# New engine orders for a two-layer attention and token-mixing kernel: the planner's DMA constants and its correction tables are replaced

## The chip, the cores and the metric

The kernel runs on one core of a Trainium2 chip. The metric is the device time of one execution in microseconds (us). Times are compared as medians of several executions. One execution was also recorded by the hardware profiler. Its "span" runs from the first to the last instruction of the program, and its own time is a little longer than its span.

## The reference, cut to what matters

Two different blocks are applied in turn, A then B, twice over (two layers with the same weights), each as a residual on a layer norm of x. Block A is attention with 32 heads of width 16 in a sliding window of 256 tokens. Block B normalises once more and mixes along the tokens: its matrices act on the token axis (2048 to 1792 and back), with a gelu between.

```python
x = x + A(_layernorm(x), wqkv, wo)        # x: 1 x 2048 x 512, bf16
x = x + B(_layernorm(x), w1, b1, w2, b2)
x = x + A(_layernorm(x), wqkv, wo)
x = x + B(_layernorm(x), w1, b1, w2, b2)
# A: H = 32, Dh = 16, W = 256
scores = einsum("bhqd,bhkd->bhqk", q, k) * Dh ** -0.5
mask = (i - j >= 0) & (i - j < W)
o = einsum("bhqk,bhkd->bhqd", softmax(where(mask, scores, -1e9)), v) @ wo
# B
u = gelu(einsum("bsd,sf->bdf", layernorm(x), w1) + b1)
y = transpose(einsum("bdf,fs->bds", u, w2) + b2)
```

## The kernel before, in words

The 2048 tokens lie in SBUF as 16 tiles of 128 tokens (t0 to t15), in four chunks of four tiles (m = 0 to 3). `STEPS` names the stages of a layer and the order in which their operations are created: p (norm, transposes, q, k and v of a chunk), a (attention of a chunk), w (output projection of a chunk), u (a chunk's share of the first token matrix) and U (the last share, with the gelu). The second token matrix, y, of layer 0 is created together with p of layer 1, so that dense matmuls of one block can stand between the attention work of the other. The y of layer 1 comes last, with the stores of the output.

Attention of a chunk is done for four groups of eight heads (o = 0 to 3). This document names such a head group by layer, chunk and group: 0.a3.o2 is layer 0, chunk 3, group 2. For each group TensorE makes four or five score pieces (line 851), ScalarE takes the exponential of each piece in two halves (863), VectorE masks them (876, 879), and TensorE multiplies with v and sums the denominators in the same matmuls (896, called pv here). Then comes a round trip that is the heart of this case, since most of it is DMA:

- VectorE copies the two PSUM banks to `cs` (940, two copies).
- SyncE (SP) issues a DMA that gathers the denominators into `rr` (942) and four DMAs that move half of the sums up by 16 partitions (946, "up").
- VectorE takes the reciprocal in `rr` (949).
- SP writes it to DRAM, `rscr` (951), and reads it back spread over partitions as `md` (954).
- GpSimd multiplies sums and reciprocals into `oT` (958).
- TensorE uses four such `oT` of a chunk in the output projection (968), and VectorE adds that to x (972).

The last group of chunk 3 takes another way without DMA (909, 923 to 927). So there are 30 round trips of seven DMAs in all.

GpSimd also makes the masked copies `kbd` of k that the scores read (783, two halves for each group, from the staging tile `stg`), small pieces of v (813), and two steps of each layer norm: `rstd` (694) and its power (696), before VectorE normalises (700). The weights of the token matrices stream in: w1 in 56 loads of 256 KB (`load_w1`, 983), used by the u matmuls (1014); w2 in 112 loads of 128 KB (`load_w2`, 994), used by the y matmuls (1037), whose result is added to x (1042).

What sets the order: every operation is created with a cost, and `schedule` plays all five engines forward on these costs. `_pick` chooses for an engine among the operations that are ready. `HOLD` and `WINDOW` decide how long TensorE prefers scores and pv over dense matmuls, and `RANK` shifts the priority of each dense matmul group (`fprio`). For a DMA the planner takes three numbers: `issue` (how long the SP queue is held), `cost` (its share of a common transfer time) and `lat` (from there to the landing). `schedule` also gives out the buffers of each pool, in its own order, and picks VectorE or ScalarE for some copies out of PSUM (`evac`, lines 734 and 736). Then `reorder` moves operations within each engine by the table `MOVES`, one list for each of TensorE, VectorE, ScalarE, GpSimd and SP. `emit` writes the queues with the waits that the data and the buffers need.

So the five queues are fixed lists. Each engine takes its list strictly in order, and an instruction that waits for a DMA holds everything behind it on that engine. In particular a reciprocal (949) that waits for `rr` holds all of VectorE, a multiply (958) that waits for `md` or an "up" holds the `kbd` and `rstd` work behind it on GpSimd, and a DMA whose input isn't ready holds all later DMAs on SP.

Of the kernel before, what the change touches and what calls it, by code (L numbers as in the profile page):

```python
# [16 lines left out]
W2F, W2OUT = 2, (3, 7)  # L17
# [4 lines left out]
    38, 478, -248, -93, 7, 6, -38, -55, 0, -12, 14, -1, -14, 17, 7, 49, 0, 0, -11, -57, -29, 12, -32, 17, 163, -113,  # L22
    -26, 0, -76, 48, 174, -114, 0, -155, 72, 0, 0, 91, 0, -197, -108, 0, -146, 0, 0, -43, -29, -200, 193, 102, 0,
    116, -16, 0, -1, 11, -60, 21, -73, 18, 2, -2, 7, 89, 40, -31, -47, -15, 10, 0, -22, -49, 42, 322, -14, 6, 33, 2,
    0, 13, 12, 0, -17, -8, -15, 0, 5, -20, 0, 0, 0, -65, 142, 93, 62, -58, 23, 23, -51, -8, -30, 20, 27, 0, -36,
    -55, 10, 8, 0, 76, 151, 136, 83, -40, -3, -176, 115, -122, 460, -486, -53, -30, 29, 53, 0, -45, 0, 0, -39, -32,
    -78, 0, -2, 0, 0, 0, 0, 0, -52, 0, 0, 0, 0, 0, 0, 0, 19, -6, -13, -12, 0, -6, 4, -18, 0, 0, 7, 132, -19, -10,
    -13, 10, 103, -116, 115, -193, 419, 0, 41, 10, 1, 0, -10, 6, -14, -46, 5, -20, 0, 0, 103, -15, 11, 17, 0, 0, -6,
    -79, -112, -156, 0, -7, 0, -468, 0, 0, 0, 2, 0, 17, -7, 9, 6, 12, 0, -28, 0, 45, 117, 31, -17, 0, 0, 0, -19, -6,
    -107, -186, 167, -24, 82, 120, 248, 217, 122, 0, -3, 18, 55, -4, -27, 0, -6, 0, -120, 0, 1, 50, 52, 478, 268, 0,  # L30
    13, 47, 0, -11, 0, 113, 15, 46, 44, -30, -22, -52, 0, 14, -410, 20, 180, -153, -435, -439, 359, -7, 0, -3, 15,
    -10, 13, 10, -4, 12, 0, -86, -10, -52, -43, 17, 227, -51, -403, -135, -167, -266, -230, -240, 44, 0, 0, 4, -190,
    72, 0, 0, 0, 0, 3, 0, -1, 0, 0, 0, 0, 0, 0, 0, 0, 0, 0, 0, 0, 0, 0, 0, 0, 0, 0, 0, 0, 0, 6, 57,
# [15 lines left out]
        0, 0, 0, 0, 0, 0, 0, 0, 0, 0, 0, 0, 0, 0, 0, 0, 0, 0, 0, 0, 0, 0, 0, 0, 0, 0, 0, 0, 0, 0, 0, 0, 0, 0, 0, 0,
        0, 0, 0, 0, 0, 0, 0, 0, 0, 0, 0, 0, 0, 0, 0, 0, 0, 0, 0, 0, 0, 0, 0, 0, 0, 0, 0, 0, 0, 0, 0, 0, 0, 0, 0, 0,  # L50
        0, 0, 0, 0, 0, 0, 0, 0, 0, 0, 0, 0, 0, 0, 0, 1, -1, 0, 0, 0, 0, 0, 0, 0, 0, 0, 0, 0, 0, 0, 0, 0, 0, 0, 0, 0,
        0, 0, 0, 0, 0, 0, 0, 0, 0, 0, 0, 0, 0, 0, 0, 0, 0, 0, 0, 0, 0, 0, 0, 0, 0, 0, 0, 0, 0, 0, 0, 0, 0, 0, 0, 0,
        0, 1, -1, 0, 1, -1, 0, 1, -1, 0, 0, 0, 0, 0, 0, 0, 0, 0, 0, 0, 0, 0, 0, 0, 0, 0, 3, -1, -1, -1, 4, 0, -2,
        -1, 2, 0, -3, 0, 0, 1, -1, 1, -1, 3, -1, 2, -2, -2, 0, 2, -1, -1, 3, -1, 2, 2, -3, 6, 6, -5, -2, -2, -2, 2,
        2, -4, 1, 4, 0, 0, 2, -1, 1, 1, 1, 1, 1, -15, 1, -1, 3, 3, 3, 20, 3, 3, 0, -7, 1, -8, -8, 16, 7, -3, 1, 1,
        15, 0, 2, 5, -9, 11, -4, -11, -11, -11, -1, -6, 0, 0, 0, 2, -10, 2, -8, 4, 11, -3, 2, -3, 1, -4, -4, 0, 4,
        6, -2, 2, -6, 6, 6, -6, -2, -1, 9, -2, -10, -3, 1, 12, -3, -3, 2, -3, 8, 2, -5, -2, -6, -3, -2, -2, 1, -3,
        5, 0, -2, -1, -1, -1, 0, 0, 0,
    ),
    (  # L60
        7, 4, 4, -2, -4, 6, 6, 6, -4, 5, 6, 4, 7, 7, 3, -7, 2, 4, 4, 4, 4, 4, 5, 10, 24, 1, 3, 13, 3, 5, 0, 1, 4,
        -30, 5, 7, -8, -28, 8, 2, -2, -6, 1, 13, -7, -1, 1, 8, -3, 5, -1, -41, -2, -2, -2, 4, -54, 3, 8, 4, -2, 4,
        -1, -1, 3, 11, -9, 4, 1, -1, 4, -7, 1, 6, 1, 6, 4, 5, -25, -1, 3, 4, 5, 6, 0, 3, 4, 4, 4, -3, 3, 3, 4, -23,
        4, 4, 4, 0, -3, 2, 2, 2, 2, -26, -32, 1, 2, 2, 2, -2, -5, 1, -1, 2, -1, -1, 0, 1, 1, 1, -3, 0, 0, 0, 0, 0,
        1, -1, 0, 0, 0, 0, 0, 0, 0, 1, -1, 0, 0, 0, 1, 1, -2, 0, 1, 1, 1, 2, 0, -5, 1, -1, 0, 2, -1, -1, 0, 2, 0, 1,
        1, 2, -5, 1, 3, 0, 0, -5, 5, 1, -1, 1, 4, 2, -6, -1, 1, 2, 0, 2, 0, 1, 1, -12, 1, 2, -2, 2, 2, 2, -2, 1, 1,
        -7, 0, 0, 0, 0, 0, 0, 0, 1, -1, 0, 0, 0, 1, 1, 1, -3, 0, 0, 0, 2, 0, 1, -3, 0, 2, 0, 1, 3, -4, 3, 3, -2, 3,
        1, 3, 4, 0, 5, 3, 7, 3, 3, 5, 5, 5, -5, -15, -9, -20, -4, 2, 2, 4, 2, 0, -5, 1, 3, -7, -1, -1, 0, 1, 3, -2,
        -1, -1, 1, -1, 0, 0, 0, 0, 0, 0, 0, 1, -1, 0, 0, 0, 1, 1, -2, 0, 0, 0, 0, 1, -1, 0, 0, 0, 0, 0, 0, 0, 0, 0,
        1, -1, 0, 0, 0, 0, 0, 0, 1, 2, 2, 2, 3, 1, -4, -7, 0, 0, 0, 0, 1, -1, 1, -1, 0, 0, 0, 0, 0, 0, 0, 0, 0, 0,  # L70
        0, 0, 0, 0, 0, 0, 0, 0, 1, -1, 2, 0, 2, 3, 3, -5, -1, 5, 3, 1, 3, -8, 2, -5, 1, -6, 0, 0, 0, 0, 0, 2, 0, -2,
        0, 2, 0, 2, -3, -1, 0, 3, -1, -1, 1, 1, 2, 2, -1, -6, 0, 1, -1, 1, 1, -2, 0, 0, 2, 3, 1, 2, 2, 2, 3, 4, 6,
        6, -10, 8, 10, -5, -13, 1, 7, 7, -1, -7, 8, -11, -9, 7, 5, 7, -6, 6, -7, -4, 4, -13, -5, -2, -8, 0, 0, 1,
        -1, 0, 0, 0, 2, 0, -2, 0, 1, 1, 1, 5, 3, 1, 3, 4, 4, 1, 3, -7, 3, 1, -14, 1, 2, 4, -1, 3, -15, -2, 1, -3, 1,
        -1, 3, -1, 2, -2, 3, 3, -1, -1, -6, 1, 2, 2, -1, 2, 2, 4, -7, 0, 0, 1, 1, 1, -8, 0, 0, 0, 0, 2, -1, -1, 0,
        0, 1, 1, -2, 0, 1, -1, 0, 0, 0, 0, 2, 0, 1, 1, 1, 1, 1, 1, 3, 6, 4, 5, 0, 8, -14, 4, 2, 5, -5, 4, 6, -4, 2,
        5, 6, 6, 3, -17, 5, 5, 2, -22, 3, 6, -9, -8, -16, 4, 5, 7, -2, 6, 6, 7, 0, 7, -9, 6, 6, 0, -5, 0, 4, -17, 1,
        2, 2, -17, -16, 0, 0, 0, 0, 0, 1, -1, 0, 2, -1, -1, 0, 0, 0, 0, 0, 0, 0, 0, 0, 0, 1, 1, 1, 1, 1, 1, 1, 1, 2,
        2, 2, -2, 1, 2, 4, 1, 1, -3, 1, 3, 3, 0, 4, 1, -4, 2, -26, 1, -3, 3, 1, -2, 1, 1, 2, 0, -6, 0, 1, 1, 2, 2,
        2, -5, -3, 2, 0, -2, 2, 2, -2, 1, 1, -4, 0, 0, 2, 0, 1, -3, 3, 0, -2, -1, 0, 0, 0, 0, 0, 3, 1, -1, -3, 2, 0,  # L80
        3, 1, -1, 1, 1, 1, 1, 5, -10, -1, 1, 2, -3, -3, 2, 0, 2, 0, -4, 0, 6, 3, 3, 4, 4, 4, 4, -7, -6, -8, 1, -8,
        0, 0, 0, 0, 0, 9, 13, -1, 18, -2, 0, 0, -3, 2, 2, -10, 2, -9, 2, 3, -8, 2, -5, -10, 3, 4, 4, -6, -3, -1, -6,
        1, 1, -2, 2, -1, 2, 0, -3, 0, 0, 0, 0, 0, 0, 3, 0, 0, -3, 0, 0, 1, 1, 3, -3, 2, -1, -3, 1, -1, 0,
    ),
# [71 lines left out]
class Graph:  # L156
# [158 lines left out]
    HOLD = 300.0  # L315
    WINDOW = ({0: 400.0, 1: 300.0, 2: 50.0}, {0: 100.0, 1: 250.0, 2: 100.0})
# [222 lines left out]
def bass_interleave_layers__sliding_block__mixer_token_mlp__prompt_kernel(  # L539
# [21 lines left out]
    with es:  # L561
# [39 lines left out]
        g = Graph(nc, es)  # L601
# [512 lines left out]
```

The softmax here doesn't subtract the row's maximum and nothing guards it: scores larger than these inputs give would overflow.

## Time and profile before

| what | us |
|---|---|
| median of 6 runs | 487.22 |
| lowest and highest of these | 483.77 and 490.5 |
| the profiled execution, its own time | 483.77 |
| its span | 482.0 |
| TensorE busy | 436.7 |
| VectorE busy | 370.7 |
| ScalarE busy | 323.4 |
| GpSimd busy | 136.6 |

The profiled execution is the lowest of the six: it took 3.45 us less than their median. A working made on its trace explains 483.77 us, and has to be carried over to the median. "Busy" of TensorE counts the time in which at least one matmul is under way. Its mean granted clock was 0.992 of full speed, so there is hardly a general clock loss, but a lower clock in a few places. In the views, PE is TensorE, PEld its weight loads, DVE VectorE, ACT ScalarE, POOL GpSimd, and SPq the issuing of DMAs on SP's queue.

### The profile page before, as it was taken

To read this page: it belongs to the slowest core of one execution; us is meant where nothing else is said; L and a number is where in the kernel's file an instruction comes from. 1 tells how busy PE (TensorE), PEld (TensorE's weight loads), DVE (VectorE), ACT (ScalarE), POOL (GpSimd) and SP (SyncE) were. 2 spreads that over 40 slices of the span, in tenths; PEclk is the share of its full clock that TensorE was granted. 3 is DMA by queue.
4 is the path that set the end of the run, shared out by engine and by line. 5 is a ranking of instruction groups with operands and counts; after the bars stand their busy time and mean duration, and the time that the engine had idled before them with its cause. 6 is when DMAs were issued, how large, how long until landed. Compare 5 with 4: busy or idle time off the path is not lost.

```text
span 482.0 us, 15699 instructions
## 1 busy us (share of the span) xinstructions
PE 436.7 (91%) x6831; PEld 208.9 (43%) x6831; DVE 370.7 (77%) x747; ACT 323.4 (67%) x367; POOL 136.6 (28%) x205
## 2 busy tenths in 40 slices
PE   7898887798888699999999999988999969999997
PEld 4453533343343244444555454434444325444443
DVE  6989978989989977665887889879996846951313
ACT  2899999999989850634878988996999852061000
POOL 4223435234521413024103433532474031200000
PEclk9999999999999999999999999998999999999999
DMA  8602221234344253331225422330345335424655
GB/s 244 183 3 73 61 85 39 65 105 130 87 112 129 59 151 89 88 88 44 78 60 137 116 67 71 89 102 9 101 112 160 83 105 162 127 71 120 175 152 176
DMA packets 83993, 49.47 MB, mean 103 GB/s; under 512 B 14676, under 2 KB 78164, under 8 KB 83924
## 3 DMA queue, kind: packets, MB, share of 16 engines
q1 hardware_dynamic: 83924, 48.46, 35.6%
q8 instruction: 54, 0.88, 0.8%
q14 instruction: 15, 0.12, 0.1%
HBM read 41.43 MB, written 2.59 MB: 91 GB/s over the span
## 4 chain that ended last, share of the span: by engine, by line
PE 63%; ACT 14%; DVE 9%; DMA 7%; SPq 3%; issue 3%; POOL 2%; POOLq 0%
PE PS L1037 18%; PE PS L1014 16%; ACT pt L863 13%; PE PS L767 7%; PE PS L851 6%; PE PS L968 5%; PE PS L896 5%; PE PS L797 4%; DVE cs L940 2%; DMA cs<-cs 2%; DVE pt L879 1%; DMA w1b<-in_B_w_dram 1%; DMA wqkv<-in_A_wqkv_dram 1%; DMA rr<-cs 1%; SPq L946 1%
## 5 line engine op out<-in xcount | busy, mean ns | idle before, releaser
L863 ACT ACTIVATE pt<-PS 128x1024 bf16<-128x1024 f32 (+1 forms) x304 | 284.3, 1032 | 37.6 <-PE PS L851 35.9
L1014 PE MATMUL PS<-xh_sb,w1b 128*128 128x512 bf16 x448 | 107.1, 382 | 6.4 <-DMA w1b<-in_B_w_dram 3.5
L1037 PE MATMUL PS<-ub,w2b 128*128 128x512 bf16 x448 | 103.6, 380 | 0.7 <-ACT pt L863 0.5
L851 PE MATMUL PS<-qT,kbd 32*128 32x64 bf16 (+4 forms) x1632 | 61.0, 244 | 18.9 <-ACT pt L863 8.6
L958 POOL TENSOR_TENSOR oT<-cs,md 128x512 bf16<-128x512 f32 x30 | 39.5, 1316 | 101.4 <-DMA md<-rscr 46.5
L1014 PEld LDWEIGHTS PS<-xh_sb,w1b 128*128 128x128 bf16 x448 | 40.3, 98 | 58.8 <-issue 9.4
L879 DVE TENSOR_TENSOR pt<-pt,ldm 128x1024 bf16<-128x1024 bf16 (+1 forms) x80 | 60.7, 760 | 5.5 <-ACT pt L863 5.2
L767 PE MATMUL PS<-xhT,wqkv 128*128 128x512 bf16 x256 | 63.2, 381 | 0.9 <-DVE cs L940 0.6
L1037 PEld LDWEIGHTS PS<-ub,w2b 128*128 128x128 bf16 x448 | 41.6, 98 | 51.2 <-issue 3.1
L783 POOL TENSOR_SCALAR kbd<-stg,par 128x512 bf16<-128x512 bf16 x56 | 46.3, 836 | 55.2 <-DVE stg L734 50.6
L1026 DVE TENSOR_TENSOR ub<-PS,ub 128x512 f32<-128x512 f32 x70 | 46.0, 682 | 15.9 <-PE PS L1014 15.7
L851 PEld LDWEIGHTS PS<-qT,kbd 32*128 32x128 bf16 x1632 | 23.4, 92 | 73.4 <-ACT pt L863 38.1
L1042 DVE SCALAR_TENSOR_TENSOR x_sb<-PS,bcol,x_sb 128x512 bf16<-128x512 f32 x32 | 23.1, 744 | 39.0 <-PE PS L1037 39.0
L1029 ACT ACTIVATE ub<-ub,bcol 128x512 bf16<-128x512 f32 x28 | 18.5, 713 | 46.8 <-DVE ub L1026 46.6
L940 DVE COPY cs<-PS 128x512 f32<-128x512 f32 x60 | 38.9, 681 | 9.0 <-PE PS L896 8.6
L896 PE MATMUL PS<-pt,vt 64*18 64x64 bf16 (+4 forms) x3040 | 39.6, 243 | 4.6 <-DVE qT L734 1.3
L694 POOL TENSOR_SCALAR rstd<-agg 128x2 f32<-128x2 f32 (+1 forms) x40 | 9.5, 237 | 120.4 <-DVE agg L691 119.4
L689 DVE BATCH_NORM_STATS2 stats<-x_sb 128x6 f32<-128x512 bf16 x64 | 42.6, 680 | 1.1 <-DMA x_sb<-in_A_x_dram 0.5
L876 DVE TENSOR_TENSOR pt<-pt,ldm 128x512 bf16<-128x512 bf16 (+1 forms) x104 | 40.2, 404 | 1.8 <-ACT pt L863 1.3
L896 PEld LDWEIGHTS PS<-pt,vt 64*18 64x18 bf16 x3040 | 31.1, 85 | 15.7 <-DVE pt L876 3.6
L968 PE MATMUL PS<-wo_sb,oT 128*128 128x512 bf16 x128 | 33.0, 389 | 3.4 <-POOL oT L958 2.8
L767 PEld LDWEIGHTS PS<-xhT,wqkv 128*128 128x128 bf16 x256 | 21.7, 98 | 29.9 <-issue 3.2
(54 smaller groups left out, 328.1 us busy)
## 6 DMA issues: line engine op xcount, KB each, us to landing
w1b<-in_B_w_dram SPq DMA_DIRECT2D x56, 256.0 KB, 3.1
w2b<-in_B_w_dram SPq DMA_DIRECT2D x112, 128.0 KB, 2.4
md<-rscr SPq DMA_DIRECT2D x30, 256.0 KB
cs<-cs SPq DMA_DIRECT2D x120, 32.0 KB, 2.7
out_dram<-x_sb SPq DMA_DIRECT2D x16, 128.0 KB, 1.8
x_sb<-in_A_x_dram SPq DMA_DIRECT2D x3, 512.0 KB
wqkv<-in_A_wqkv_dram SPq DMA_DIRECT2D x2, 384.0 KB
x_sb<-in_A_x_dram SPq DMA_DIRECT2D x4, 128.0 KB, 2.4
```

What stands on the lines that cost most here:

```text
L689: op("vector", lambda e, t=t: e.bn_stats(stats[:, t, :], x_sb[:, t, :]), reads=[f"x{t}"], writes=[f"st{t}"], cost=dve_cost(512))
L767: mm_group(ft, 4, lambda e, c: e.matmul(PS[:, ft.slot, :], lhsT=wqkv[:, c, which * 512 + o * P:which * 512 + (o + 1) * P], rhs=xhT[:, tx.s ...
L783: op("gpsimd", lambda e, h=h: e.tensor_scalar(kbd[:, tk[o].slot, :, h, :], stg[:, ts.slot, :].rearrange("p (s n) -> p s n", n=64), par[:, ...
L851: last = e.matmul(PS[:, bank(r), c0 * 64:(c0 + nb) * 64], lhsT=kbd[32 * r:32 * r + 32, tkk.slot, jj, :, :].rearrange("p h n -> p (h n)"), ...
L863: return e.activation(pt[:, tp.slot, 2 * u:2 * u + 2, 0:n], PS[:, b0:b0 + 2, 0:n], ACTF.Exp, scale=SMSCALE)
L879: return e.tensor_tensor(v, v, msk.unsqueeze(1).unsqueeze(1).to_broadcast([P, 4, k, w]), op=ALU.mult)
L896: last = e.matmul(PS[32 * r:32 * r + 18, tO[h].slot, q0 * 64:(q0 + nb) * 64], lhsT=vt[64 * h:64 * h + 64, tvv.slot, jj, 4 * o + r, :], rhs ...
L940: op("vector", lambda e, tO=tO[h], tc=tc, h=h: e.tensor_copy(cs[:, tc.slot, h], PS[:, tO.slot, :]), reads=[tO[h]], writes=[(tc, h)], cost= ...
L968: mm_group(ft, 4, lambda e, o, i=i, ft=ft: e.matmul(PS[:, ft.slot, :], lhsT=oT[:, tos[o][0].slot, i * P:(i + 1) * P], rhs=wo_sb[:, o, :], ...
L1014: out_ = e.matmul(PS[:, tu.slot, :], lhsT=w1b[:, tw.slot, s, tt * P:(tt + 1) * P], rhs=xh_sb[:, 4 * m + s, :], start=(n == 0 and s == 0), ...
L1026: op("vector", lambda e, tu=tu, ft=ft: e.tensor_tensor(uacc(ft), PS[:, tu.slot, :], uacc(ft), op=ALU.add), reads=[tu] + uk(ft), writes=uk( ...
L1037: mm_group(ft, NFT, lambda e, fc: e.matmul(PS[:, ft.slot, :], lhsT=w2b[:, tws[fc // W2F].slot, fc % W2F, k * P:(k + 1) * P], rhs=uT(fc), s ...
```

## The change

No line that computes anything is touched. Three sorts of numbers are replaced:

- The planner's numbers for DMAs, as below.
- `HOLD` and `WINDOW`, as below.
- The tables `RANK` (322 entries, of which 182 differ) and `MOVES` (717, 747, 367, 201 and 409 entries for TensorE, VectorE, ScalarE, GpSimd and SP). Their entries are plain shifts without a meaning of their own.

```diff
-    HOLD = 300.0
-    WINDOW = ({0: 400.0, 1: 300.0, 2: 50.0}, {0: 100.0, 1: 250.0, 2: 100.0})
+    HOLD = 600.0
+    WINDOW = ({0: 400.0, 1: 300.0, 2: 0.0}, {0: 150.0, 1: 400.0, 2: 400.0})
...
                     # rr <- cs
-                   writes=[(tr, 0)], dma=True, cost=300, lat=1400.0, issue=570.0, prio=len(g.ops))
+                   writes=[(tr, 0)], dma=True, cost=200, lat=1400.0, issue=610.0, prio=len(g.ops))
                     # cs <- cs, the four "up"
-                       writes=[(tc, "up", r)], dma=True, cost=120, lat=1600.0, issue=380.0, prio=len(g.ops), after=[o_rr])
+                       writes=[(tc, "up", r)], dma=True, cost=120, lat=1850.0, issue=575.0, prio=len(g.ops), after=[o_rr])
                     # rscr <- rr
-                   writes=[te], dma=True, cost=300, issue=580.0, prio=len(g.ops))
+                   writes=[te], dma=True, cost=200, lat=1500.0, issue=400.0, prio=len(g.ops))
                     # md <- rscr
-                   writes=[tm], dma=True, cost=700, lat=2500.0, issue=590.0, prio=len(g.ops))
+                   writes=[tm], dma=True, cost=700, lat=2650.0, issue=645.0, prio=len(g.ops))
                     # w1b
-               dma=True, cost=1000, lat=2000.0, issue=390.0, prio=1e6 + len(g.ops))
+               dma=True, cost=1000, lat=1900.0, issue=450.0, prio=1e6 + len(g.ops))
                     # w2b
-                    cost=340 * W2F, lat=1700.0, issue=390.0, prio=1e6 + len(g.ops), after=w2_sent[-W2OUT[g.layer]:][:1]))
+                    cost=340 * W2F, lat=1400.0, issue=480.0, prio=1e6 + len(g.ops), after=w2_sent[-W2OUT[g.layer]:][:1]))
                     # out_dram
-            op("sync", lambda e, t=t: e.dma_start(out_v[:, t, :], x_sb[:, t, :]), reads=[f"x{t}"], dma=True, cost=600,
+            op("sync", lambda e, t=t: e.dma_start(out_v[:, t, :], x_sb[:, t, :]), reads=[f"x{t}"], dma=True, cost=500, lat=1000.0,
```

What this does to the program can be read from the two instruction lists. Both hold the same operations: 717 groups of matmuls on TensorE (of them 14 single warm-up matmuls), 747 on VectorE, 367 on ScalarE, 201 on GpSimd and 409 on SP. Nine copies out of PSUM go from VectorE to ScalarE and nine the other way. What differs is the order: the same operation stands at the same place of the list in 152 of 717 places on TensorE, 64 of 747 on VectorE, 111 of 367 on ScalarE, 41 of 201 on GpSimd and 41 of 409 on SP. Buffers of the pools are given out in the new order too.

## The prediction, made before the changed kernel was run

> **What bounds the kernel now.** I read the page's busy times first, then the busy times by stretch, then the table of waits, then the timeline at the longest stops of TensorE.
>
> ```profile
> PE 436.7 (91%) x6831; PEld 208.9 (43%) x6831; DVE 370.7 (77%) x747; ACT 323.4 (67%) x367; POOL 136.6 (28%) x205
> ```
>
> TensorE is busy for 436.7 of 482.0 us, so at most 45 us are idle, and the work on it is the same after the change. Only part of the idle time can be won: the start costs 2.4 us, and the stages differ. The columns below are the stretch, its length, and each engine's busy time in it, then the granted clock.
>
> ```profile
> 40.00:60.00 20.00, 17.03 (x361) 9.34 (x362) 18.99 (x44) 19.87 (x24) 7.30 (x9) 1.00 0.29 78
> 80.00:100.00 20.00, 15.66 (x432) 8.94 (x433) 17.68 (x34) 19.54 (x22) 7.81 (x8) 1.00 0.26 68
> 260.00:280.00 20.00, 18.74 (x366) 8.76 (x362) 16.62 (x32) 17.21 (x21) 11.19 (x12) 1.00 0.43 110
> 320.00:340.00 20.00, 17.52 (x286) 8.36 (x286) 16.69 (x33) 15.15 (x16) 4.88 (x6) 0.91 0.23 67
> 380.00:400.00 20.00, 15.86 (x300) 7.41 (x296) 12.57 (x28) 12.08 (x14) 5.16 (x7) 0.91 0.45 123
> ```
>
> In layer 0 (first two rows) ScalarE is full, at 19.5 to 19.9 of 20 us: there a stop of TensorE costs less than its length, and one of ScalarE costs all of it. In layer 1 (the others) TensorE is nearest to full, and its stops count in full. Two of these rows show a clock of 0.91. The waits (us in total, times, longest) say what TensorE and VectorE stopped for:
>
> ```profile
> DVE rr L949 <- DMA rr<-cs: 8.9, 5, 5.1
> PE PS L1014 <- DMA w1b<-in_B_w_dram: 3.5, 1, 3.5
> DVE xh_sb L700 <- POOL rstd L696: 3.5, 6, 1.3
> PE PS L968 <- POOL oT L958: 2.8, 3, 2.2
> PE PS L750 <- DVE x_sb L1042: 2.1, 1, 2.1
> ```
>
> Four of these five end with a landing DMA or with something that stood behind one (the multiply L958, or the add L1042 behind a reciprocal). The timeline gives the places (start, length, and the idle time before it in brackets):
>
> ```profile
> 181.89 1.04 PE L968 MATMUL PS<-wo_sb,oT 128*128 128x512 bf16 x4 [2.15 <-POOL oT L958]
> 325.35 0.35 DVE L949 RECIPROCAL rr<-rr 128x32 f32<-128x32 f32 x1 [2.12 <-DMA rr<-cs]
> 326.32 0.40 PE L750 MATMUL PS<-ident,xh_sb 128*128 128x128 bf16 x4 [2.11 <-DVE x_sb L1042]
> 395.00 2.65 PE L1014 MATMUL PS<-xh_sb,w1b 128*128 128x512 bf16 x8 [3.46 <-DMA w1b<-in_B_w_dram]
> 395.24 0.35 DVE L949 RECIPROCAL rr<-rr 128x32 f32<-128x32 f32 x1 [5.12 <-DMA rr<-cs]
> ```
>
> The second and third line are one event: the reciprocal waits on VectorE, the add L1042 stands behind it, and TensorE waits for the add. So the chip stops where a DMA lands late and too little work stands between its issue and its user.
>
> **The change part by part.** No work is added or removed. What moves is order, so each part is priced by cover: how much work the consumer's own engine has between the producer and the consumer. I counted it in both instruction lists, with durations from this trace: each VectorE instruction by its own time, on TensorE 0.86 us for four 512-column matmuls (76 of L1014 took 16.40 us), 1.35 for a pv group, 0.36 for a score piece.
>
> *Planner numbers.* They cost nothing by themselves. The trace shows which of them fit: median issue lengths are 604 ns for rr, 571 for an "up", 413 for rscr, 647 for md. A round trip holds SP for 0.604 + 4 x 0.571 + 0.413 + 0.647 = 3.95 us. The old numbers say 3.26, the new ones 3.96. Over 30 round trips the old plan was 30 x 0.69 = 21 us short on SP, the new one is not. This is why the new covers can be expected where the chip needs them.
>
> *Reciprocals (VectorE, past the copies 940).* The mean cover over layer 1's 15 round trips goes from 4.2 to 6.4 us, in layer 0 from 5.3 to 5.8. Covers under 3 us fall from 9 to 3 of 30. At the stop at 325 (1.a2.o0) the reciprocal came 4.9 us after the copies. Its cover goes from 3.0 to 7.7 us, so such a landing is hidden. TensorE gains 2.1 us.
>
> *The clock behind that stop.* [...]
>
> ```profile
> 328.00:330.00 2.00, 2.00 (x17) 0.67 (x16) 1.92 (x5) 1.34 (x2) 0.48 (x2) 0.50 0.00 0
> 330.00:332.00 2.00, 2.00 (x116) 1.34 (x115) 1.29 (x2) 0.60 (x1) 0.40 (x1) 0.72 0.03 8
> 396.00:397.00 1.00, 1.00 (x4) 0.30 (x2) 0.82 (x2) 0.00 (x0) 0.99 (x3) 0.50 0.20 41
> ```
>
> Behind the 2.11 us stop the clock fell to 0.50 and 0.72: 2 x 0.50 + 2 x 0.28 + 2 x 0.07 (the 2 us before had 0.93) = 1.7 us of TensorE work lost. [...] At 395 to 400 it is 0.5 + 0.5 + 2 x 0.35 = 1.7 us again. At 182 the clock stayed 1.00.
>
> *End of layer 0's attention (0.a3.o2).* TensorE's cover from pv to the projection goes from 11.8 to 13.6 us, and the last "up" stands 9 instead of 11 SP issues behind rr, about 1 us earlier. The 2.15 us stop is covered, and dense matmuls follow without a break: gain 2.1 us.
>
> *w1 loads.* At 395 TensorE waited for a load issued at 388.5. Covers of the loads just there (layer 1, u of chunks 0 and 1, blocks 2 to 4) go from 4.2, 4.7 and 5.1 us to 6.3, 6.3 and 7.6. Of 3.46 us about 2.1 are covered; the clock's 1.7 us I count half, since a gap of 1.4 remains. Gain 3.0 us, between 1.6 (the least-moved load, no clock) and 5.2.
>
> *GpSimd.* At 81 us two kbd halves (1.96 us) stand between the two steps of one rstd, and VectorE waits 1.26 us for it. In the new list the two steps stand together. TensorE stops of 1.59 and 1.73 us lie around it. Gain 0.6 us, between 0 and 1.3, as ScalarE is the full engine there.
>
> *Remaining reciprocal waits*, 8.9 - 5.1 - 2.1 = 1.7 us on VectorE: 0.5 us.
>
> *The start.* Two more warm-up matmuls (0.43 us each here) stand ahead of the first transpose: 0.9 us later. The wqkv loads behind two waits of 0.3 and 0.6 us move ahead of a 512 KB load of x on SP, but the two bias loads (0.86 and 0.88 us of issue) move ahead of them. They read 7.5 KB, so the bytes ahead get fewer; first scores now also need three k and q groups instead of four (0.9 us). Sum 0, from -1 to +1.
>
> *A thinner cover (0.p3.k2).* In the new list the second kbd half of chunk 3's group 2 stands on GpSimd behind the multiply of 0.a2.o3 (before: behind that of 0.a2.o1). From that pv to the first score that needs it there are 13.7 us of TensorE work, where there were over 30. The way is 1.3 (copies) + 12.2 (copies to multiply, as now) + 1.3 + 0.6 + 2 x 0.8 = 17.0 us. At TensorE's share of 0.82 busy in that stretch 13.7 us of work last 16.6. It is 0.4 us late: cost 0.5, more if that landing is late.
>
> *Late landings elsewhere.* Other covers shrink (reciprocals of 0.a1.o1 from 10.6 to 7.0 and of 0.a1.o2 from 7.7 to 4.9 us; the least cover of a projection in layer 0 from 6.2 to 5.7, counting from the last TensorE work that its inputs depend on). Landing times vary: an "up" took 1.9 to 6.0 us, median 2.7. I charge one event of the middle size, 3.8 us, between 0 and two (7.6).
>
> The sum against the profiled execution: -2.1 - 2.1 - 1.7 - 3.0 - 0.6 - 0.5 + 0 + 0.5 + 3.8 = -5.7 us, 483.8 to 478.1. The other runs are longer by 3.45 us in the median; as the program is the same they probably met more late landings. I carry the difference over whole: 487.2 - 5.7 = **481.5 us**.
>
> **Rivals.**
> *Late landings were accidents of that execution.* [...] Then the GpSimd order, the small waits and about a third of the 182 us stop (0.7, for the earlier issue) are left: -0.7 - 0.6 - 0.5 + 0.5 = -1.3, so 485.9 us. [...]
> *The orders are equal on the chip:* as many stops as before, in other places, 487 us. For it: both lists have the same dense work ahead of the first and last score to within about 2 us, so the coarse plan is the same. Against it: the fewer thin covers.
> *Slower: the k half behind the multiply.* If the landings of 0.a2.o3 come late by 3.3 us (6.0 instead of 2.7), the scores of 0.a3.o2 stop for 0.4 + 3.3 = 3.7 us; ScalarE, which is full there, empties, and the clock falls for another 1.7: 5.4 us. With no gain elsewhere this is 492.6 us. It decides once scores stand still for over 5 us beyond what the other parts gain. For it: nine of GpSimd's waits for md reach 6.3 us at the longest. Against it: one place only.
> The change could also fail to do what it says; the lists show that it moves nearly every queue, so that isn't likely.
>
> **How the numbers follow.** Covers hold: 0.55, around 481.5, its own range 476.5 to 486. Accidents: 0.10, at 485.9. Equal: 0.10, at 487. Slower: 0.25, 488 to 496. The low end, 476, is the sum with all of the w1 event won and one late landing less (-5.7 - 2.2 - 3.8 = -11.7, so 475.5); the high end, 491.5, cuts the slower case so that about 2 in 10 stay outside. One per cent (482.3 or 492.1, about what a measurement of this kernel can tell from no change): faster 0.37 from the first case and 0.04 from the next two; slower by over 1%, 0.24; the rest within.
>
> **What would show it.** Right: the waits of the reciprocals on rr well under 8.9 us; no TensorE stop over 2 us before 968, 750 or 1014 with a DMA or multiply behind it; clock 1.00 from 320 to 400. Wrong: ScalarE idle before the scores of 0.a3.o2 around 150 us; VectorE waiting for rr as long in other places; TensorE busy but longer by more than 2 us, which would mean clock.

## The result and the profile after

The changed kernel took 482.68 us (median of 34 runs, 479.3 to 486.79), the kernel before beside it 485.98 us (71 runs): ratio 0.9938, 95% interval [0.9921, 0.9955]. A second comparison, on another chip, gave 484.28 us (12 runs) beside 487.27 us (29 runs), ratio 0.9982 [0.9944, 1.0020]: again 3.0 us between the medians, but an interval that holds 1. (The ratios leave out runs more than 1.5% above the fastest of their kernel, in the second comparison 11 of the 29 of before and none of the changed kernel, so they are not the quotients of the medians.) The gain is 3.0 to 3.3 us between the medians, a little over half of the 5.7 us that the sum had. The profiled execution took 480.72 us, its span was 479.0 us, and its mean granted clock 1.000 instead of 0.992.

Busy times of the changed kernel, first part of its page:

```profile
PE 434.0 (91%) x6831; PEld 207.7 (43%) x6831; DVE 368.2 (77%) x747; ACT 323.5 (68%) x367; POOL 132.0 (28%) x205
```

Subtract from the span: TensorE is idle for 479.0 - 434.0 = 45.0 us. In before it was 482.0 - 436.7 = 45.3 us. **The stops that the forecast wanted to remove are gone, and the idle time is not.** What shrank is the busy time, by 2.7 us: before's trace has two stretches of 3.4 us at a granted clock of 0.5, in which the same matmuls last longer, and the changed kernel's has none before its last matmul.

Busy times of the changed kernel from 320 to 400 us (TensorE, its weight loads, VectorE, ScalarE and GpSimd, then the granted clock, the DMA share and GB/s); the two middle stretches are added:

```profile
320.00:340.00 20.00, 17.95 (x317) 9.07 (x316) 19.90 (x41) 17.25 (x19) 5.24 (x7) 1.00 0.20 61
340.00:360.00 20.00, 17.63 (x378) 8.46 (x377) 18.08 (x35) 14.47 (x16) 11.35 (x18) 1.00 0.30 79
360.00:380.00 20.00, 18.29 (x383) 8.32 (x382) 14.83 (x28) 17.44 (x19) 5.34 (x6) 1.00 0.46 128
380.00:400.00 20.00, 18.24 (x343) 8.57 (x340) 15.33 (x28) 15.42 (x17) 4.77 (x7) 1.00 0.50 144
```

The same two added stretches of before:

```profile
340.00:360.00 20.00, 18.61 (x408) 9.17 (x403) 18.87 (x39) 18.20 (x20) 11.93 (x17) 1.00 0.36 100
360.00:380.00 20.00, 19.59 (x392) 8.58 (x393) 14.84 (x26) 17.67 (x19) 6.68 (x7) 1.00 0.40 111
```

TensorE's idle time (20 less its first column) from 320 to 400 us goes from 2.48 + 1.39 + 0.41 + 4.14 = 8.42 us to 2.05 + 2.37 + 1.71 + 1.76 = 7.89 us. The stretches with the stops won 2.8 us, the two between them lost 2.3. VectorE is now full from 320 to 340 us (19.90 of 20).

Waits of the changed kernel (us in total, times, longest):

```profile
DVE xh_sb L700 <- POOL rstd L696: 3.4, 5, 1.5
...
DVE rr L949 <- DMA rr<-cs: 1.2, 2, 0.9
...
PE PS L968 <- POOL oT L958: 0.8, 1, 0.8
...
PE PS L1014 <- DMA w1b<-in_B_w_dram: 0.4, 1, 0.4
```

The waits of reciprocals for rr fell from 8.9 to 1.2 us, those for w1b from 3.5 to 0.4, those of the projections from 2.8 to 0.8. The places of the old stops, and the longest stop past the start, in the timeline of the changed kernel (idle time before in brackets):

```profile
181.85 1.46 PE L968 MATMUL PS<-wo_sb,oT 128*128 128x512 bf16 x6
326.80 0.74 DVE L734 COPY xhT<-PS 128x512 bf16<-128x512 bf16 x2
327.35 0.40 PE L851 MATMUL PS<-qT,kbd 32*128 32x64 bf16 x12 [1.70 <-DVE xhT L734]
328.06 0.33 DVE L949 RECIPROCAL rr<-rr 128x32 f32<-128x32 f32 x1
388.08 1.02 PE L1014 MATMUL PS<-xh_sb,w1b 128*128 128x512 bf16 x4 [0.43 <-DMA w1b<-in_B_w_dram]
391.53 2.76 PE L1014 MATMUL PS<-xh_sb,w1b 128*128 128x512 bf16 x12
```

Three stops of 2.15, 2.11 and 3.46 us became none, 1.70 (in front of other work) and none. Followed along the two traces, the first gelu of layer 0 starts 1.1 us earlier (193.62 to 192.54), the first exponential of layer 1 at the same time (223.48, 223.76). A count of the work done (TensorE's busy time, each part times its granted clock, an estimate from the two traces) shows where the 3.0 us come from. The changed kernel is 2.0 us ahead at 340 us, behind the stop and the low clock that before has there. At 380 us it is 0.3 us behind, at 392 us 0.1 behind, at 396 us 2.1 ahead and at 400 us 3.8 ahead. So the first lead was lost again, and what stays is won between 392 and 400 us: about 2 us by the stop and 1.7 by the clock behind it.

**Why DMAs landed late there.** DMA issues on SP around the stop at 395 us, in before:

```profile
387.15 1.33 SPq L954 DMA_DIRECT2D md<-rscr  x2
388.52 0.45 SPq L983 DMA_DIRECT2D w1b<-in_B_w_dram  x1
389.02 0.56 SPq L946 DMA_DIRECT2D cs<-cs  x1
389.68 0.57 SPq L942 DMA_DIRECT2D rr<-cs  x1
395.24 0.57 SPq L946 DMA_DIRECT2D cs<-cs  x1
```

and in the changed kernel:

```profile
383.91 0.64 SPq L954 DMA_DIRECT2D md<-rscr  x1
384.83 1.35 SPq L983 DMA_DIRECT2D w1b<-in_B_w_dram  x2
386.23 0.53 SPq L946 DMA_DIRECT2D cs<-cs  x1
387.05 0.65 SPq L954 DMA_DIRECT2D md<-rscr  x1
387.74 1.17 SPq L946 DMA_DIRECT2D cs<-cs  x2
389.02 0.62 SPq L942 DMA_DIRECT2D rr<-cs  x1
```

In before, two reads of md stand back to back, and behind them a half load of w1, an "up" and rr. By the semaphore events of the trace these five landed 3.9, 6.2, 6.3, 6.0 and 5.5 us after issue, and SP stood still from 390.25 to 395.24, since an "up" waits for rr. In the changed kernel the two md reads are 3.1 us apart, and w1 and rr landed after 4.8 and 3.4 us. The rr that the sum saw landing late at 325 us has the same neighbourhood: md reads at 318.59 and 319.35, rr at 321.20, landed after 4.1 us; the changed kernel issues that rr between its two md reads, and it landed after 1.96 us. All 330 rr of eleven profiles (all but b_sp, a_sp and b_fill395) say the same:

| md reads issued in the 3 us before an rr | rr | median us to landing | 10% to 90% |
|---|---|---|---|
| none | 249 | 2.0 | 1.95 to 2.2 |
| one | 69 | 2.6 | 2.0 to 3.4 |
| two | 12 | 4.1 | 3.2 to 4.5 |

Before's profile has 24, 3 and 3 of these, the changed kernel's 20, 10 and none. So late landings are not accidents: they come where the list puts reads close ahead. Loads of w1 do the same (past 20 us: median 3.1 us with no md read issued in the 3 us before, 3.8 with one, 5.7 with two; 484, 107 and 8 loads). Weight loads add to the delay, but they are not its cause alone: with no md read, one weight load ahead leaves an rr at 2.0 us (69 of them) and two go with 3.0 (12), while two md reads without a weight load go with 3.4 (6).

In the trace an md read shows 9 semaphore events and an rr 5 (all 30 of each in before). Whether the counts have to do with the delay is not shown: the trace has the counts and the landing times, and where on its way an rr is held was not tried by itself.

### The profile page after: what moved, and what is told of

Same layout as the page of the kernel before. It is cut to its first block, busy times and chain, and to the rows that moved or that the text cites. A ratio compares the mean times of both kernels' runs of the same rounds, so it can differ in the third digit from the quotient of the medians.

```text
span 479.0 us, 15719 instructions
## 1 busy us (share of the span) xinstructions
PE 434.0 (91%) x6831; PEld 207.7 (43%) x6831; DVE 368.2 (77%) x747; ACT 323.5 (68%) x367; POOL 132.0 (28%) x205
## 4 chain that ended last, share of the span: by engine, by line
PE 56%; DVE 16%; ACT 15%; DMA 5%; POOL 3%; SPq 2%; issue 2%; POOLq 0%
PE PS L1037 19%; PE PS L1014 15%; ACT pt L863 14%; PE PS L767 5%; PE PS L851 5%; PE PS L896 4%; PE PS L797 3%; PE PS L968 3%; DVE pt L876 2%; DVE cs L940 2%; DVE pt L879 2%; DMA rscr<-rr 2%; POOL kbd L783 2%; DVE qT L734 2%; DMA x_sb<-in_A_x_dram 1%
## 5 line engine op out<-in xcount | busy, mean ns | idle before, releaser
L783 POOL TENSOR_SCALAR kbd<-stg,par 128x512 bf16<-128x512 bf16 x56 | 43.5, 786 | 59.7 <-DVE stg L734 37.8
L879 DVE TENSOR_TENSOR pt<-pt,ldm 128x1024 bf16<-128x1024 bf16 (+1 forms) x80 | 55.6, 704 | 2.9 <-ACT pt L863 2.9
L1026 DVE TENSOR_TENSOR ub<-PS,ub 128x512 f32<-128x512 f32 x70 | 45.3, 683 | 15.8 <-PE PS L1014 15.7
L876 DVE TENSOR_TENSOR pt<-pt,ldm 128x512 bf16<-128x512 bf16 (+1 forms) x104 | 42.6, 429 | 2.2 <-ACT pt L863 1.7
L797 PE MATMUL PS<-wqkv,xhT 128*64 128x256 bf16 x512 | 33.3, 275 | 2.1 <-DVE cs L940 1.0
```

The costliest lines, as they stand in the source:

```text
L783: op("gpsimd", lambda e, h=h: e.tensor_scalar(kbd[:, tk[o].slot, :, h, :], stg[:, ts.slot, :].rearrange("p (s n) -> p s n", n=64), par[:, ...
L797: last = e.matmul(PS[64 * hf:64 * hf + 64, ft.slot, sc * 256:(sc + 1) * 256], lhsT=xhT[:, tx.slot, c, tok:tok + 64], rhs=wqkv[:, c, 1024:1 ...
L876: return e.tensor_tensor(v, v, msk.unsqueeze(1).to_broadcast([P, 4, w]), op=ALU.mult)
L879: return e.tensor_tensor(v, v, msk.unsqueeze(1).unsqueeze(1).to_broadcast([P, 4, k, w]), op=ALU.mult)
L1026: op("vector", lambda e, tu=tu, ft=ft: e.tensor_tensor(uacc(ft), PS[:, tu.slot, :], uacc(ft), op=ALU.add), reads=[tu] + uk(ft), writes=uk( ...
```

## The experiments

Theory Q: landings are late by queueing behind the kernel's own md reads, and the new order gains by spreading them. Theory C: it gains by longer covers of the reciprocals. Theory E: the orders are equal, stops only move. Each variant is timed against before on the same chip. The names of the runs begin with b_ for changes to the kernel before and with a_ for changes to the changed kernel.

**One load, and the md reads.** `put(e, i, where, j)` moves one operation next to another in an engine's list. The load alone:

```diff
+        put("sync", 1852, "after", 1853)   # w1, block 6, second half
```

> The kernel before with one DMA moved: the second w1 load of layer 1's block 6 goes up four places on SP, ahead of an 'up' and of two md reads. Theory Q (landings are late because they queue behind the kernel's own md reads): the load lands before TensorE needs it, the 3.46 us stop at 395 and about 1.7 us of lower clock go, minus what the late rr still holds: 1 to 4 us faster, and the rr behind the two md reads still lands 4.5 to 5.5 us after its issue. Theory C (the gain of the changed kernel is its longer covers at many places): cover in TensorE work is not changed here, 0 to 1 us faster. Theory E (the orders are equal and stops only move): no change.

Measured: 0.9978 [0.9939, 1.0017]; the VectorE waits for rr were 9.7 us, longest 4.3. The 3.46 us stop for w1 went down to 1.27, and a stop of 2.27 us with another releaser came up 4 us later. The moved load, now with two md reads behind it instead of ahead, still took 5.2 us from issue to landing. So the load alone gains nothing that can be told.

The load and three md reads, each behind the rr that it stood ahead of:

```diff
+        put("sync", 1852, "after", 1853)
+        put("sync", 2109, "after", 2134)   # md of 1.a3.o1 behind rr of 1.a3.o2
+        put("sync", 1690, "after", 1883)   # md of 1.a1.o3 behind rr of 1.a2.o0
+        put("sync", 773, "after", 798)
```

> As the run with the load moved up, and at three places (0.a2.o3, 1.a2.o0, 1.a3.o2) the second of two md reads goes behind the rr gather that it preceded on SP. Covers on VectorE are those of the kernel before. Theory Q: the three rr land after 2.0 to 3.4 us instead of 3.5, 4.1 and 5.5, the stops at 325 and 395 go, 2 to 5 us faster, so about all that the changed kernel gains. Theory C: the thin covers (2.2 to 3.0 us) stay and keep most of the waits, at most 1 us faster. Theory E: no change, other stops take the place.

Measured: 0.9961 [0.9929, 0.9992]. Its waits:

```profile
PE PS L909 <- POOL vb L813: 3.4, 1, 3.4
DVE rr L949 <- DMA rr<-cs: 3.2, 2, 2.7
```

and its GpSimd timeline around the old stop at 395 us:

```profile
396.08 1.26 POOL L958 TENSOR_TENSOR oT<-cs,md 128x512 bf16<-128x512 f32 x1 [5.19 <-DMA md<-rscr]
397.43 0.19 POOL L694 TENSOR_SCALAR rstd<-agg 128x2 f32<-128x2 f32 x1
397.71 0.37 POOL L813 TENSOR_SCALAR vb<-vt,half 128x128 bf16<-128x128 bf16 x1
```

No rr has two md reads ahead any more, and the waits for rr fell from 8.9 to 3.2 us. This is Q's direction, at the low end of its forecast. But GpSimd waited 5.2 us for md, and the step vb (L813), whose input had been ready for over 50 us, stood behind the waiting multiply: TensorE waited 3.4 us for that instead of 3.5 for w1. (In before the multiply waits 4.80 us and vb comes at 396.0 us, hidden behind the stop for w1.) E is right at this place. The changed kernel has vb ahead of that multiply, which the sum did not count:

```profile
381.55 0.37 POOL L813 TENSOR_SCALAR vb<-vt,half 128x128 bf16<-128x128 bf16 x1
388.45 1.27 POOL L958 TENSOR_TENSOR oT<-cs,md 128x512 bf16<-128x512 f32 x1 [5.88 <-DMA md<-rscr]
```

So at 395 us the changed kernel has both: w1 in time on SP, and vb made before the wait on GpSimd. The place of vb was not tried by itself.

**Covers alone.** Three reciprocals, each behind later work on VectorE, SP as before:

```diff
+        put("vector", 1888, "after", 1722)   # 1.a2.o0
+        put("vector", 2139, "after", 2162)   # 1.a3.o2
+        put("vector", 803, "after", 656)
```

> The kernel before with the order on SP as it was, and three reciprocals (0.a2.o3, 1.a2.o0, 1.a3.o2) moved back on VectorE past 1.1 to 2.6 us more of its work. Theory C: the waits at these places shrink by that much, 1 to 3 us faster. Theory Q: the landings stay late (3.5, 4.1, 5.5 us), SP still stands still behind the last of them and the w1 load is as late as before: within 1 us of before. Theory E: no change.

Measured: 1.0035 [0.9993, 1.0077]. The waits for rr fell to 3.5 us, nearly as far as in b_unpair, and yet nothing was won. TensorE stopped for 3.48 us at 396.29 (w1b), and at the place of the old stop at 326 us:

```profile
326.99 0.33 DVE L949 RECIPROCAL rr<-rr 128x32 f32<-128x32 f32 x1
328.06 1.87 PE L968 MATMUL PS<-wo_sb,oT 128*128 128x512 bf16 x4 [2.13 <-POOL oT L958]
```

The reciprocal no longer waits, but rr lands no sooner, and the projection, which needs it by way of md and the multiply, stops TensorE instead. Theory C falls for these three places of the old order.

**The changed kernel with md reads paired again:**

```diff
+        put("sync", 1658, "before", 1883)
+        put("sync", 2077, "before", 2109)
+        put("sync", 1852, "after", 2109)
```

> The changed kernel with the md reads put back in pairs right ahead of an rr gather at two places (1.a2.o0 and 1.a3.o2), and one w1 load behind the second pair, as the kernel before has them. Its covers stay. Theory Q: these two rr land after 4 to 5.5 us and the w1 load after over 5, 2 to 4 us slower than the changed kernel, which takes its gain away: 0 to 1 us faster than the kernel before. Theory C: the covers of 7.7 us at 1.a2.o0 and those elsewhere hold most of it, 2 to 3 us faster than before, as the changed kernel is. Theory E: as the changed kernel, too.

Measured: 0.9957 [0.9916, 0.9998]. At 1.a2.o0 the rr landed after 4.1 us again, at 1.a3.o2 after 3.1; a w1b stop of 1.04 us came back at 395.9. So the landings are Q's. The time is not: Q had 0 to 1 us faster than before, and 0.9957 is where C and E had it, though the interval reaches to Q. The first of the two late landings cost nothing, because the long cover was there:

```profile
331.10 0.33 DVE L949 RECIPROCAL rr<-rr 128x32 f32<-128x32 f32 x1
```

This reciprocal came 2.7 us behind the landing and did not wait; the other waited 2.73 us, and vb stayed ahead of its multiply, at 384.1 us. So unpairing the reads gains in the old order, and pairing them again costs nothing that can be told in the new one.

**Whole lists.** The next two swap SP's list between the kernels:

```diff
+        g.order["sync"] = g.ranked("sync", SYNC_ORDER)   # the other kernel's 409 issues
```

> The kernel before with SyncE's whole instruction list taken from the changed kernel (all 409 DMA issues in the new order); TensorE, VectorE, ScalarE and GpSimd keep their old lists. The changed kernel measured 0.994 against before. Theory Q (the gain is that reads of md no longer stand close ahead of rr and of the late weight loads on SP): most of it comes with this list alone, 0.994 to 0.998, rr landings at the three former places back to 2.0 to 3.5 us, no VectorE wait for rr over 2.5 us. Rival G (the gain needs the lists of the computing engines, so that the queue fits them): 1.000 or slower, up to 1.01, since SP's new order serves engines that still work in the old order, and new waits of TensorE for w1b or of VectorE for rr come up.

> The changed kernel with SyncE's list of the kernel before (22 of its 409 places repaired, where buffers forbid the old place); the other engines keep the new lists. Theory Q: the gain is gone, 0.998 to 1.003 against before, with rr landings of 3.5 us and more behind pairs of md reads. Rival G (lists of the computing engines): the gain stays, 0.993 to 0.996, because the covers of reciprocals and of the projections stay as large as in the changed kernel and hide the late landings.

Measured: 1.064 [1.056, 1.072] and 1.089 [1.082, 1.097]. Neither theory had that size. Waits of before with the new SP list (its lines are 27 higher, so L976 is L949 and L995 is L968):

```profile
DVE rr L976 <- DMA rr<-cs: 15.7, 6, 7.9
...
PE PS L995 <- POOL oT L985: 8.5, 3, 4.0
PE PS L794 <- DVE cs L967: 8.0, 3, 6.8
```

A list that fits its own partners costs 33 and 48 us (between the medians) with others. By the mean clocks of the runs (0.960 and 0.956, where before has 0.991) 16 and 19 us of this are a lower clock. That SP issues wait at the head of the queue for engines with other work first is likely, but not shown: SP's waits for the copies to `cs` are 31.7 us in before with the new list and 28.4 us in the changed kernel itself. The orders cannot be priced engine by engine, as the sum did.

**GpSimd's rstd order.** The moves of b_unpair and one more:

```diff
+        put("gpsimd", 386, "after", 385)   # second step of the rstd directly behind its first
```

> The kernel before with five single moves: the late half load of w1 four places earlier, three md reads behind the rr that they stood ahead of (these four alone measured 0.9961 [0.9929, 0.9992]), and the second step of the one rstd at 81 us directly behind its first step on GpSimd. If the GpSimd order is worth what the prediction gave it (0.6 us) and adds up: 0.995 with the TensorE stops of 1.59 and 1.8 us at 83 and 88 us down to about 1.0 and 1.3; then this and the reads together are nearly the whole change (0.9938). If ScalarE, full in that stretch, sets the pace, the two stops shrink and the time stays at 0.996.

Measured: 0.9959 [0.9925, 0.9993]. The stops of TensorE at 83 and 88 us are as they were:

```profile
83.86 0.40 PE L851 MATMUL PS<-qT,kbd 32*128 32x64 bf16 x12 [1.59 <-DVE qT L734]
87.59 0.40 PE L851 MATMUL PS<-qT,kbd 32*128 32x64 bf16 x12 [1.65 <-ACT pt L863]
```

VectorE's wait of 1.26 us for the rstd at 84 us is gone, and nothing came of it: the new place of the rstd step is worth nothing there that can be told.

**The thin cover of 0.p3.k2.**

```diff
+        put("gpsimd", 576, "before", 806)   # in the changed kernel: half block ahead of the multiply of 0.a2.o3
```

> The changed kernel with the one half block of chunk 3's k group 2 moved back ahead of the multiply of head 0.a2.o3 on GpSimd (the thin cover that the prediction charged with 0.5 us, and on which its slower rival rested). If that cover is what holds the changed kernel at 145 to 154 us: 0.9925 to 0.993 against before, and the stop of 0.8 us on TensorE at 151 us and those of 1.5 and 0.9 us on ScalarE near by are gone. If it is not: 0.9938 as the changed kernel, and they stay.

Measured: 0.9991 [0.9958, 1.0025]. TensorE's stop of 0.79 us is gone, another of 0.92 came at 145, and ScalarE's stops of 1.47 and 0.89 us became one of 1.94. The medians are 481.81 us and 484.51 us for before, so 2.7 us apart, where the changed kernel has 3.3 and 3.0. That cover is not what holds the changed kernel.

**What a stop does to the clock.** Busy times of before in windows of 3.41 us around its two drops:

```profile
324.30:327.71 3.41, 1.18 (x8) 0.55 (x8) 2.37 (x6) 1.68 (x2) 3.33 (x4) 1.00 0.09 17
327.71:331.12 3.41, 3.41 (x66) 1.31 (x72) 2.86 (x8) 1.94 (x2) 0.88 (x2) 0.50 0.00 0
331.12:334.53 3.41, 3.25 (x120) 2.00 (x106) 3.06 (x7) 2.08 (x3) 0.00 (x0) 1.00 0.02 5
392.57:395.98 3.41, 0.98 (x5) 0.52 (x6) 0.74 (x3) 0.00 (x0) 1.68 (x2) 1.00 0.14 30
395.98:399.39 3.41, 3.41 (x57) 1.74 (x58) 2.49 (x6) 0.00 (x0) 2.25 (x3) 0.50 0.35 90
```

The granted clock is third from last. Each drop is 0.50 for one window (1.7 us of TensorE work), and it follows a window in which TensorE was busy for 1.18 and 0.98 of 3.41 us. The two drops start 68.27 us apart, 20 windows. Every run states its span and its mean clock over it, so that the lost time of a run is (1 - clock) x span: a drop of 1.7 us takes 0.0035 off the mean. (The texts on record took 432 us in place of the span, so their figures for the lost clock are a tenth too small.) This gives a second measure, the span less the lost clock, called the rest below. Means over all runs with standard errors, in us; where before stands in a row, the variants below it ran on the same chip:

| kernel | runs | lost clock | span less lost clock |
|---|---|---|---|
| changed (first comparison) | 35 | 2.7 ± 0.3 | 478.6 ± 0.2 |
| before | 35 | 5.0 ± 0.3 | 479.4 ± 0.3 |
| before + load (b_load_up) | 12 | 4.6 ± 0.9 | 480.4 ± 0.5 |
| before + load and md moves (b_unpair) | 12 | 5.4 ± 0.6 | 477.9 ± 0.3 |
| before + covers (b_cover) | 12 | 6.9 ± 0.6 | 479.7 ± 0.5 |
| before | 23 | 4.4 ± 0.4 | 478.0 ± 0.3 |
| before + five moves (b_fix) | 12 | 3.8 ± 0.5 | 476.5 ± 0.5 |
| changed, thin cover undone (a_thin) | 12 | 3.5 ± 0.7 | 477.4 ± 0.4 |
| before | 29 | 5.1 ± 0.3 | 479.8 ± 0.3 |
| changed, again (a_again) | 12 | 3.4 ± 0.5 | 479.0 ± 0.4 |
| before + three fillers (b_fill) | 12 | 1.6 ± 0.4 | 483.1 ± 0.4 |
| before + thirteen moves (b_best) | 12 | 3.1 ± 0.5 | 476.8 ± 0.4 |
| before | 17 | 4.7 ± 0.5 | 479.6 ± 0.5 |
| before + one filler (b_fill395) | 12 | 2.5 ± 0.5 | 480.6 ± 0.5 |

The first row has no clocks of before from its own chip. a_pair is left out: of its 12 executions two took 1461 us, for a reason that is not known, and a third had a mean clock of 0.946. The load and md moves shorten the rest by 1.5 us, in b_unpair and in b_fix alike, and leave the clock within its errors. The changed kernel unaltered:

> The changed kernel unaltered, to read its clock and its span on the same chip as before and the two kernels beside it. So far [...]the runs' mean clocks give 2.4 us lost per run for the changed kernel and 4.0 to 4.5 us for before. Theory H (about half of the gain is fewer clock drops, the other half a shorter schedule): ratio 0.992 to 0.996; lost clock 1.5 to 2.5 us less than before; span less lost clock 0.5 to 1.5 us less than before's. Rival I (the gain is schedule alone, the clock a coincidence of few runs): lost clock equal to before's within 0.7 us.

Against before on the same chip the lost clock goes from 5.1 to 3.4 us and the rest is 0.9 ± 0.5 us shorter: H, as far as it goes together. Its profiled execution agrees with the first one: rr waits of 0.9 us, no stop over 1 us at 182 and 395 us, one of 1.52 at 330. Whether the clock is a cause was tried by filling the stops with matmuls of zeros into PSUM banks that are overwritten next:

```diff
+        fill(987, 987, 5)     # at the stop at 182 us
+        fill(1730, 1782, 6)   # at the stop at 326 us
+        fill(1854, 1854, 9)   # at the stop at 395 us
```

> The kernel before with TensorE kept busy in three of its stops: 5 matmuls of zeros (1.1 us) ahead of the projection 0.w3.0 that stops at 182 us, 6 (1.3 us) ahead of the transposes that stop at 326 us, 9 (1.9 us) ahead of the w1 product that stops at 395 us, each into a PSUM bank that the next product there overwrites. All orders and all DMAs stay, so the late landings stay late. Theory H: the stops no longer empty a 3.41 us window, the clock stays up there, lost clock falls from about 4.2 to 1.5 to 2.5 us per run, and the time from 1.000 to 0.995 to 0.997. Rival L (only the length of the stops counts, the clock follows something else): lost clock unchanged, 1.000 or slower by the part of the fillers that no stop hides, up to 1.004.

Measured: 1.0017 [0.9982, 1.0052]. Its timeline at two stops:

```profile
347.86 0.26 PE L851 MATMUL PS<-qT,kbd 32*128 32x192 bf16 x2 [1.44 <-issue]
...
392.80 2.10 PE L616 MATMUL PS<-zero 128*128 128x512 bf16 x9
396.06 1.89 PE L1014 MATMUL PS<-xh_sb,w1b 128*128 128x512 bf16 x7 [1.15 <-DMA w1b<-in_B_w_dram]
```

The fillers do hold the clock (lost 1.6 us instead of 5.1), so it is the stop that drops it. But the time is not shorter: the rest is 3.3 us longer. In the two profiles b_fill is 1.4 us behind before at the stop at 326 us and 0.1 us behind at 346, as before has its low clock between. At 348 us it is 1.8 us behind again, behind a stop of 1.44 us that before does not have and for which the profile shows no releaser. One filler alone, the last:

```diff
+        fill(1854, 1854, 9)
```

> The kernel before with the 9 matmuls of zeros (1.9 us) at the w1 product that stops TensorE at 395 us, and no others. That stop was 3.5 us in before and 1.15 us behind the fillers, so the fillers lie wholly inside it, and what they change is the clock behind it alone. Theory H (a clock drop lies on the path): lost clock 1.0 to 1.7 us less than before's per run, span less lost clock equal to before's within 0.6 us, time 0.997. Rival E (what the clock gives is waited away later, as it looked with three fillers): lost clock also less by 1.0 to 1.7 us, but span less lost clock longer by as much, time 1.000 within 0.3%.

Measured: 1.0000 [0.9972, 1.0029]; over all runs the lost clock is 2.2 us less and the rest 1.0 ± 0.8 us longer, so that their mean is 1.2 ± 0.8 us shorter. That lies between H and E. How much of a restored clock reaches the end stays open; no filler made a kernel faster clear of noise.

**A version to beat both.** b_fix and eight more moves, after the lines of b_unpair and b_fix above:

```diff
+        put("sync", 2292, "after", 1690)    # w2 load behind rr and md
+        put("sync", 1805, "after", 2292)    # w1 load likewise
+        put("gpsimd", 2000, "after", 2009)  # rstd, vb, rstd ahead of a multiply that waits for md
+        put("gpsimd", 1745, "after", 2000)
+        put("gpsimd", 2001, "after", 1745)
+        put("gpsimd", 2078, "before", 2110) # multiply of 1.a3.o0 ahead of that of 1.a3.o1
+        put("gpsimd", 1536, "before", 1659)
+        put("gpsimd", 1537, "before", 1659)
```

> A version to beat both kernels: before with the five moves of the earlier run (0.9959) and eight more: two weight loads behind the md read and the rr of 1.a2.o0 that they delayed, and on GpSimd five steps that were ready for 5 to 50 us moved ahead of a multiply that waits for a late md read, and the multiply of 1.a3.o0 ahead of that of 1.a3.o1. Theory Q (queueing on SP and on GpSimd behind md reads is what stops TensorE): 0.990 to 0.993, the stop of 2.3 us at 398 gone, that of 2.1 us at 329 under 1.2 us. Rival E (stops only move): 0.995 to 0.997 as without the eight, with the idle time of TensorE within 1 us of 45.

Measured: 0.9927 [0.9881, 0.9972], 481.41 us beside 484.28 us for the changed kernel on that chip. The intervals of the two overlap, but the rest is shorter by 2.2 ± 0.6 us. Its GpSimd timeline at the old stop:

```profile
387.93 0.38 POOL L813 TENSOR_SCALAR vb<-vt,half 128x128 bf16<-128x128 bf16 x1
388.27 0.69 POOL L696 TENSOR_TENSOR rstd<-rstd,mhalf 128x2 f32<-128x2 f32 x1
391.30 2.67 POOL L958 TENSOR_TENSOR oT<-cs,md 128x512 bf16<-128x512 f32 x2 [2.34 <-DMA cs<-cs]
```

vb is made at 387.9 us and both multiplies are done at 394.0, where b_unpair had 397.7 and 400.0. The time is what Q forecast, but its stops did not go as it said: one of 2.83 us remains at 394.3, now behind VectorE's mask, and the one before the projection, forecast under 1.2 us, is 1.91 at 326.34. So thirteen single moves do as much as the new set of orders, perhaps more; which of the eight new ones did it was not tried.

## Why the prediction was right in sign and half right in size

481.5 us was forecast, 482.68 measured, inside the range. Part of that agreement is luck: over 71 runs before's median is 485.98 us, not 487.22, and from there the sum would have said 480.3. The sum had -5.7 us; the medians differ by 3.3 and 3.0 us. **The step that failed is in the reading of the stretches: "In layer 1 (the others) TensorE is nearest to full, and its stops count in full."** Three stops of 7.7 us went, and TensorE's idle time went from 45.3 to 45.0 us, since other engines stopped it elsewhere. Term by term:

- *0.a3.o2 at 182 us, -2.1:* the stop is gone, as said. The first gelu came 1.1 us sooner, and at 223 us nothing of it was left. The working counted a removed stop as time won, without the next stage.
- *Reciprocals, -2.1 and -0.5:* the wait is gone (8.9 to 1.2 us). That the new cover hides such a landing was right: a_pair shows it at this place. But the changed kernel did not need it, as its rr landed after 1.96 us, issued ahead of the second md read. And "TensorE gains 2.1 us" did not follow: a stop of 1.70 us at 327.35 took the old one's place, behind a copy on VectorE, which has no time left from 320 to 340 us. In b_cover, too, the stop only moved, to the projection. The lead of 2.0 us at 340 us, most of it the clock's, was gone at 380.
- *Clock, -1.7 here and 0.85 within the next term:* drops of 1.7 us each were priced rightly, and the profiled execution lost none. Over runs the changed kernel still loses 2.7 to 3.4 us, on the same chip 1.7 us less than before, not 3.4. Whether all of that is a gain was not shown.
- *w1 at 395 us, -3.0:* this stop was won, and is where the 3.0 us of the profiles come from. But the load was taken for one of "blocks 2 to 4". It is the second half of block 6, whose cover is 6.3 us in both lists. It landed late behind two md reads, and moving that load alone gave 0.9978 [0.9939, 1.0017]. GpSimd's order (vb), which the sum counted at 81 us only, has a part in it: where w1 came in time and vb did not, in b_unpair, a stop of 3.4 us stayed.
- *GpSimd, -0.6:* 0 in b_fix, within what its interval can tell; both stops stayed.
- *Thin cover, +0.5:* undoing it did not make the kernel faster. The slower rival, which rested on it, did not come.
- *Late landings elsewhere, +3.8:* an allowance for one random event. There was no such event in the profile: no rr landed later than 3.4 us, and no "up" later than 4.9. What was given back was given back in other waits, 2.3 us of TensorE from 340 to 380 us alone. That the sum came out near is partly this: a term for something else stood in for it.

Of the rivals, "accidents" is refuted by the table of landings: in all five profiles with two md reads close ahead of an rr at these places (before, b_load_up, b_cover, a_pair, b_fill) an rr landed after 4.1 to 5.5 us. "Equal" was nearer than its chance of 0.10: idle time of TensorE is 45.3 and 45.0 us. Counting the clock behind the 2.11 us stop was right: before's granted clock is 0.50 for 3.41 us there.

## What to carry over

In these traces an rr landed after a median of 2.0 us where the same queue had issued no md read in the 3 us before it, and after 4.1 us where it had issued two, so look at the neighbours of a late DMA before adding cover: in the old order, moving reads behind the small transfers that somebody waits for helped (with one load, 0.9961), and waiting later alone did not (1.0035). On an in-order engine, put what has long been ready ahead of what waits for a DMA: in b_unpair vb stood behind a multiply that waited 5.2 us for md, and TensorE stopped 3.4 us for it. And price a removed stop from the idle time that is left afterwards, not from the stop: here three stops of 7.7 us went and 0.3 us of idle time.

## What the runs showed of the hardware

The granted clock falls to 0.50 in these traces for windows of 3.41 us, and within an execution the drops start whole windows apart: 20 in before, 17 and 10 in a_pair (at 28.60, 86.63 and 120.76 us). Each drop lasts one window, except in the two kernels with exchanged lists, where some last longer: in a_sp four matmuls of 512 columns took 1.87 us at 155.98 us and 112 of pv 2.16 us at 160.14 us, against 1.04 and 1.36 us later in the same trace. So the "every drop" of the expectation for a_again holds without these two kernels alone.

Ten profiles have a drop between 10 and 470 us (the exchanged lists left out). In these, between the same times, every window with TensorE busy for up to 0.45 of it was followed by a drop, 16 in all (shares of 0.35 and 0.29 in before, 0.44 in a_pair, 0.42 in b_fix, 0.28 in a_thin, 0.44 in b_fill, 0.40 in b_best among them); five more drops followed shares of 0.48 to 0.58, and the lowest share without one was 0.47, in b_fix. Before's first window, from 0.03 us, had a share of 0.32 and no drop behind it. In b_fill395, whose windows can be placed only by a drop at its very end, one window of 0.44 had none. So these profiles show no sharp limit: below 0.44 the clock fell each time past the start, and up to 0.58 it sometimes did.

A stop of 2.1 us drops the clock or does not: in before one of 2.11 us at 326 us did and one of 2.15 us at 182 us did not, and in b_fill395 one of 2.56 us at 328.30 us did not. Over 35 runs the same program (the changed kernel) loses anything from 0 to 7.3 us. That this comes from how a stop falls on the windows, which begin 1.88 and 1.54 us into the span in the changed kernel's two profiled executions, is likely and was not tried.
